# Four K=32 row strips for the gated products of a fused attention and GEGLU kernel, with re-made instruction tables

## The chip, the cores and the metric

One core of one Trainium2 chip. The metric is device time of one execution in microseconds. All runs quoted are of the fast state; on one core, executions of one kernel mostly agree within 0.3%. A ratio of two kernels is the mean time of the fast runs of one over the mean of the fast runs of the other in the same rounds on the same chip, so it is not quite the ratio of the medians quoted beside it.

## The reference, cut to what matters

```python
# x: 4 x 12416 x 128, inducing: 32 x 128
h = mab(I, x)            # 32 rows attend to all of x: h is 32 x 128 for each of 4 batches
y = mab(x, h)            # every x row attends to the 32 rows of h: y = a @ h, a is 12416 x 32
# then on the 49664 rows of y:
ffn = (gelu(y @ w_gate) * (y @ w_val)) @ w_out      # 128 -> 1536 -> 128
out = y + sigmoid(y @ w_res) * ffn
```

Since y = a @ h with only 32 columns in a, the kernel never forms y for the first layer: it computes h @ w_gate and h @ w_val once per batch (32 x 1536 each) and multiplies the attention weights a with them. So the inner dimension K of the large products is 32.

## The kernel before

A *slot* is 512 tokens x 2 chunks of 128 hidden columns: two gate halves (each one matmul with 512 columns into a `g` bank), two value halves (into a `v` pair of banks), two gelus on ACT, and one multiplication on DVE that gives `u` (1,024 columns). Six slots make a group of 512 tokens. TensorE (PE) then multiplies `u` with w_out in 48 small matmuls, called f here, into the single `f` bank. 146 slots make a batch, four batches the kernel. While batch b runs, the exponentials, sums and first layer of batch b+1 run in the background, in slots 90 to 125 or so.

Partitions 0 to 31 and 32 to 63 of the weights both hold the gate copy, 64 to 127 the value copy twice. Before, one product used two copies at once (K=64), and the scales 0.5 and 0.25 undid the doubling:

```python
def emit(gate, value):              # one gate half and one value half
    todo = []
    if gate is not None:
        gb = bank_g()               # 3 banks
        todo.append(products(*gate, slice(0, 64), gb))
    if value is not None:
        ...                         # v: two pairs of banks
        todo.append(products(i, h, slice(64, 128), v_t[i][:, h * TOK:(h + 1) * TOK]))
    ...                             # the matmuls, in turn; then gelu (ACT), and after the 2nd half u (DVE)
```

The mixes (R: input of the sigmoid, written as tanh; A: the residual) used half the height:

```python
pe.matmul(bank[...], rt_t[...][rows, ...], hra_t[self.b][rows, :])    # rows = 0:64 or 64:128
```

The order of all this is a table of words, one word a slot. P: the two value halves with two gate halves; Q: with one gate half; V: without; G: one gate half alone; a number: so many f matmuls; R, A: mixes; E: 16 blocks of exponentials; c, h, t, l, r, o: other steps of the next batch. A star at a row's end makes ACT copy the f bank (and GpSimd, POOL, do the rest); without a star DVE does `(th + 1) * f` from the bank. Two rows of the middle table, before:

```python
"8P9 P R10P QE4 EE23EEEcE2cP cQG2",
"GP9 P A8P QG8 2GP 11PA *",
```

The softmax here doesn't subtract the row's maximum and nothing guards it: scores larger than these inputs give would overflow.

## Time and profile before

| | before |
|---|---|
| median of 3 runs | 802.83 us (801.81 to 803.2) |
| first u starts, last u starts | 38.1, 796.3 us |
| the four batches (first u to first u, the last to its last u) | 201.1, 190.0, 189.9, 177.2 us |

The batch times are read from the starts of the u instructions in the trace. The first batch contains a hole near 143 to 151 us. The page's lines are shown in the prediction. ACT's records are about 0.64 us long but can start every 0.477 us, so ACT can be 99% "busy" and still be late.

### The profile page before, as it was taken

The numbers are of one execution on the slowest core, as the hardware profiler recorded it, in microseconds if no ns is written. First come the engines' busy times: TensorE is split into PE (matmuls) and PEld (weight loads), VectorE is DVE, ScalarE is ACT, GpSimd is POOL, SyncE is SP. The second block draws the span as 40 slices with busy tenths as digits, with TensorE's granted clock in tenths as the row PEclk, the third lists the DMA queues.
The fourth block names the chain that finished last, engine by engine and source line by source line (L and its number), as shares of the span: only waits on it lengthen the run. The fifth ranks groups of instructions, "written<-read, shape, count | busy, mean of one in ns | idle before, by whom it ended". The sixth has DMA issues, their size and how long they took to land.

```text
span 801.7 us, 23912 instructions
## 1 busy us (share of the span) xinstructions
PE 771.1 (96%) x9590; PEld 477.3 (60%) x9590; DVE 736.4 (92%) x714; ACT 771.8 (96%) x1528; POOL 518.7 (65%) x504
## 2 busy tenths in 40 slices
PE   5899999699999999999999999999999999999997
PEld 4556556465665656565666655566666565565655
DVE  7799999389899999979899999997989999999997
ACT  7799999599999999999999999999999999999997
POOL 0338998533888999852587999971388683433545
PEclk9999999799999999999999999999999999999999
DMA  9315579411044657710025565651014441101111
GB/s 349 97 44 137 148 183 199 78 45 41 28 98 99 148 145 177 193 61 28 28 74 97 130 149 148 188 122 39 29 35 100 89 96 41 40 28 41 40 41 45
DMA packets 118449, 78.16 MB, mean 97 GB/s; under 512 B 96672, under 2 KB 99392, under 8 KB 118336
## 3 DMA queue, kind: packets, MB, share of 16 engines
q1 hardware_dynamic: 118336, 76.62, 37.2%
q8 instruction: 75, 1.23, 0.7%
q14 instruction: 38, 0.31, 0.1%
HBM read 27.87 MB, written 25.43 MB: 66 GB/s over the span
## 4 chain that ended last, share of the span: by engine, by line
PE 72%; ACT 19%; issue 4%; DMA 2%; DVE 2%; POOL 1%; SPq 0%; DVEq 0%; POOLq 0%; ACTq 0%
PE f L389 31%; PE g L352 28%; ACT ge L358 12%; PE g L397 5%; PE v L352 3%; ACT at L408 1%; ACT xt L142 1%; DMA xf<-in_x_dram 1%; DVE u L366 1%; ACT e L167 1%; ACT fe L417 1%; PE g L163 1%; ACT th L403 1%; PE g L181 1%; ACT hi L117 1%
## 5 line engine op out<-in xcount | busy, mean ns | idle before, releaser
L366 DVE TENSOR_TENSOR u<-ge,v 128x1024 bf16<-128x1024 f32 x584 | 679.1, 1212 | 39.3 <-PE v L352 20.9
L358 ACT ACTIVATE ge<-g 128x512 f32<-128x512 f32 x1164 | 609.3, 641 | 5.4 <-PE v L352 2.1
L352 PE MATMUL g<-rt,hgv 64*128 64x512 f16 x1152 | 360.1, 380 | 3.0 <-DVE nacc L191 0.4
L389 PE MATMUL f<-wO,u 128*128 128x128 bf16 x4656 | 358.7, 221 | 3.0 <-DVE th L421 1.3
L352 PE MATMUL v<-rt,hgv 64*128 64x512 f16 x1152 | 359.4, 383 | 0.0
L389 PEld LDWEIGHTS <-u 128*128 128x128 bf16 x4656 | 265.9, 98 | 134.6 <-issue 119.7
L352 PEld LDWEIGHTS <-hgv 64*128 64x128 bf16 x2400 | 124.8, 93 | 112.2 <-issue 36.2
L422 POOL TENSOR_TENSOR at<-at,th 128x512 f32<-128x512 f32 (+1 forms) x100 | 123.9, 1240 | 81.8 <-ACT ge L358 48.6
L418 POOL TENSOR_TENSOR th<-th,fe 128x512 f32<-128x512 f32 (+1 forms) x58 | 70.6, 1218 | 118.9 <-ACT fe L417 118.7
L293 POOL TENSOR_TENSOR a<-e,z 128x1024 f16<-128x1024 f32 (+1 forms) x48 | 89.7, 1878 | 14.6 <-DVE z L279 9.7
L397 PE MATMUL g<-hra,rt 64*128 64x128 f16 x768 | 73.2, 216 | 8.7 <-ACT e L167 7.6
L397 PEld LDWEIGHTS <-rt 64*128 64x128 f16 x768 | 51.1, 94 | 47.1 <-issue 27.2
L125 POOL TENSOR_TENSOR lo<-xf,hi 128x1024 f16<-128x1024 f32 x36 | 76.9, 2136 | 0.3
L419 POOL TENSOR_TENSOR at<-at,fe 128x512 f32<-128x512 f32 (+1 forms) x58 | 70.6, 1218 | 0.0
L408 ACT ACTIVATE at<-g 128x512 f32<-128x512 f32 (+1 forms) x100 | 61.8, 618 | 0.3 <-issue 0.2
L403 ACT ACTIVATE th<-g 128x512 f32<-128x512 f32 (+1 forms) x100 | 61.7, 618 | 0.4
L119 POOL CAST hi<-xf 128x1024 f16<-128x1024 f32 x36 | 37.4, 1038 | 14.0 <-DMA xf<-in_x_dram 11.2
L417 ACT ACTIVATE fe<-f 128x512 f32<-128x512 f32 (+1 forms) x58 | 36.0, 621 | 2.1 <-PE f L389 2.0
L421 DVE SCALAR_TENSOR_TENSOR th<-th,f 128x512 f32<-128x512 f32 x42 | 28.6, 681 | 1.6 <-POOL a L272 1.6
L163 PEld LDWEIGHTS <-xt 128*128 128x128 f16 x768 | 23.3, 97 | 8.0 <-issue 3.9
L206 POOL CAST hra<-hf 64x128 f16<-64x128 f32 x4 | 1.1, 288 | 40.4 <-DVE hf L201 30.1
L167 ACT ACTIVATE e<-g 128x512 f16<-128x512 f32 (+1 forms) x36 | 18.5, 613 | 8.0 <-POOL a L293 7.9
(112 smaller groups left out, 281.1 us busy)
## 6 DMA issues: line engine op xcount, KB each, us to landing
out_dram<-at SPq DMA_DIRECT2D x96, 256.0 KB, 2.0
xf<-in_x_dram SPq DMA_DIRECT2D x38, 512.0 KB, 4.3
ge<-in_x_dram SPq DMA_DIRECT2D x10, 512.0 KB, 7.8
rt<-a SPq DMA_TRANSPOSE x48, 3.1
xt<-hi SPq DMA_TRANSPOSE x36, 3.4
ge<-in_moe_w_gate_dram SPq DMA_DIRECT2D x1, 512.0 KB, 8.8
ge<-in_moe_w_val_dram SPq DMA_DIRECT2D x1, 512.0 KB, 8.9
ge<-in_moe_w_out_dram SPq DMA_DIRECT2D x1, 512.0 KB, 4.3
```

Of the source, the lines that this page charges most:

```text
L125: eng.tensor_tensor(lo[:, :w, :P], xf_t.pop((b, k))[:, :w, :], hi_t[b, k][:, :w, :], AL.subtract)
L293: eng.tensor_tensor(a2[:, :n], ev[:, o:o + n, :].unsqueeze(2).to_broadcast([P, n, Q, M]), z[:, o:o + n].unsqueeze(2).unsqueeze(3).to_broad ...
L352: pe.matmul(*t[n], start=True, stop=True)
L358: act.activation(ge_t[i][:, h * TOK:h * TOK + n], gb[:, :n], AC.Gelu, bias=0.0, scale=1.0)
L366: ve.tensor_tensor(u[:, :n], ge_t.pop(i)[:, :n], v_t.pop(i)[:, :n], AL.mult)
L389: pe.matmul(self.ffn[:, k, :], u_t[self.gi, si][:, o:o + P], wO[:, fc, :], start=first, stop=not self.todo, skip_group_check=True)
L397: pe.matmul(bank[:, k * P:(k + 1) * P], rt_t[self.b, self.k][rows, self.j0 + k, :], hra_t[self.b][rows, :], start=True, stop=True)
L403: act.activation(self.th[:, :self.tw], self.mix(slice(0, 64)), AC.Tanh, bias=0.0, scale=0.5)
L408: act.activation(self.at[:, :self.tw], self.mix(slice(64, 128)), AC.Copy, bias=0.0, scale=1.0)
L418: po.tensor_tensor(th, th, fe, AL.mult)
L419: po.tensor_tensor(at, at, fe, AL.add)
L422: po.tensor_tensor(at, at, th, AL.add)
```

## The change

The intent: use each copy once. With K=32 four products on four different row strips can run in the array at once, where two ran before. The scales double, the mixes use all 128 rows with zeros in the unused ones (the same array mode as the f matmuls), and the tables were made anew for the lighter PE, with 35 stars in place of 58.

```diff
-    def products(i, h, rows, bank):
+    def products(i, h, strip, bank):
+        rows = slice(strip * M, (strip + 1) * M)          # M = 32
...
-    def emit(gate, value):
+    def emit(value, ngate):
         todo = []
-        if gate is not None:
-            gb = bank_g()
-            todo.append(products(*gate, slice(0, 64), gb))
         if value is not None:
+            v = v_t[value] = bank_v()
+            for h in range(len(halves_of(value))):
+                todo.append(products(value, h, 2 + h, v[:, h * TOK:(h + 1) * TOK]))
+        for _ in range(ngate):
+            ...
+                gb = bank_g()
+                todo.append(products(*gate, sent["g"] % 2, gb))
... (matmuls in turn, then u on DVE, then the gelus on ACT)
-        hra = p_h.tile([P, P], FP16, ...)
+        hra = p_h.tile([P, 2, P], FP16, ...)               # two versions, each with 64 zero rows
...
-    pe.matmul(bank[...], rt_t[...][rows, ...], hra_t[self.b][rows, :])
+    pe.matmul(bank[...], rt_t[...][:, ...], hra_t[self.b][:, s, :])
...
-                at(8 * i - 4, lambda i=i: weights_b(0, i))
-            for i, j in zip((16, 46, 80), later):
+                at(6 * i - 2, lambda i=i: weights_b(0, i))
+            for i, j in zip((14, 38, 62), later):
... (all three tables; the row of the middle table with the first exponentials:)
-        "8P9 P R10P QE4 EE23EEEcE2cP cQG2",
+        "R9GQ 19EEEV VE EE6EccQ G9P 7VGG6 *",
```

More of the change, by code (lines that the diff above doesn't have):

```diff
@@ L199, in finish_h @@
         ve.reciprocal(rz, hs[:, P:P + 1])
-        hf = p_h.tile([P, P], FP32, name="hf", tag="hf", bufs=1)
+        hf = p_h.tile([P, P + 1], FP32, name="nacc", tag="nacc", bufs=1)[:, :P]
         ve.tensor_scalar(hf, hs[:, 0:P], rz, None, op0=AL.mult)
         hf_t[b] = hf
-        hra = p_h.tile([P, P], FP16, name="hra", tag="hra")
+        hra = p_h.tile([P, 2, P], FP16, name="hra", tag="hra")
         hra_t[b] = hra
-        po.tensor_copy(hra[2 * M:, :], hf[2 * M:, :])
-        po.tensor_tensor(hra[3 * M:, :], hf[3 * M:, :], hra[3 * M:, :], AL.subtract)
+        po.memset(hra[2 * M:, 0, :], 0.0)
+        po.memset(hra[:2 * M, 1, :], 0.0)
+        po.tensor_copy(hra[2 * M:, 1, :], hf[2 * M:, :])
+        po.tensor_tensor(hra[3 * M:, 1, :], hf[3 * M:, :], hra[3 * M:, 1, :], AL.subtract)
         hgv_t[b] = p_h.tile([P, F], BF16, name="hgv", tag="hgv")
@@ L236, in first_layer_t @@
         act.activation(hgt_t[b][:, s].rearrange("p c m -> p (c m)"), bank[:, :FCH * M],
-                       AC.Copy, bias=0.0, scale=(0.5, 0.25)[s])
+                       AC.Copy, bias=0.0, scale=(1.0, 0.5)[s])
     def spread(b, c0, c1):
@@ L252, in res_layer @@
         hra = hra_t[b]
-        act.activation(hra[:64, :], bank[:64, :P], AC.Copy, bias=0.0, scale=1.0)
-        ve.tensor_tensor(hra[M:2 * M, :], bank[M:2 * M, :P], hra[M:2 * M, :], AL.subtract)
+        act.activation(hra[:64, 0, :], bank[:64, :P], AC.Copy, bias=0.0, scale=1.0)
+        ve.tensor_tensor(hra[M:2 * M, 0, :], bank[M:2 * M, :P], hra[M:2 * M, 0, :], AL.subtract)
     def sums_b(b, j0, j1, eng):
@@ L336 @@
     v_t = {}
-    def emit(gate, value):
+    def emit(value, ngate):
         todo = []
-        if gate is not None:
-            gb = bank_g()
-            todo.append(products(*gate, slice(0, 64), gb))
         if value is not None:
-            i, h = value
-            if h == 0:
-                v_t[i] = bank_v()
-            todo.append(products(i, h, slice(64, 128), v_t[i][:, h * TOK:(h + 1) * TOK]))
-        for n in range(max(map(len, todo))):
+            v = v_t[value] = bank_v()
+            for h in range(len(halves_of(value))):
+                todo.append(products(value, h, 2 + h, v[:, h * TOK:(h + 1) * TOK]))
+        gates = []
+        for _ in range(ngate):
+            gate = gate_half()
+            if gate is not None:
+                gb = bank_g()
+                todo.append(products(*gate, sent["g"] % 2, gb))
+                gates.append((gate, gb, len(todo[-1])))
+        for n in range(max(map(len, todo), default=0)):
             for t in todo:
@@ L352, in emit @@
                     pe.matmul(*t[n], start=True, stop=True)
-        if gate is not None:
-            i, h = gate
+        if value is not None:
+            gi, si = flat[value]
+            n = groups[gi][4][si][1] * groups[gi][3] * P
+            u = p_u.tile([P, 2 * TOK], BF16, name="u", tag="u")
+            ve.tensor_tensor(u[:, :n], ge_t.pop(value)[:, :n], v_t.pop(value)[:, :n], AL.mult)
+            u_t[gi, si] = u
+        for (i, h), gb, n in gates:
             if h == 0:
                 ge_t[i] = p_ge.tile([P, 2 * TOK], FP32, name="ge", tag="ge")
-            n = len(todo[0]) * groups[flat[i][0]][3] * P
+            n *= groups[flat[i][0]][3] * P
             act.activation(ge_t[i][:, h * TOK:h * TOK + n], gb[:, :n], AC.Gelu,
                            bias=0.0, scale=1.0)
-        if value is not None:
-            i, h = value
-            if h == len(halves_of(i)) - 1:
-                gi, si = flat[i]
-                n = groups[gi][4][si][1] * groups[gi][3] * P
-                u = p_u.tile([P, 2 * TOK], BF16, name="u", tag="u")
-                ve.tensor_tensor(u[:, :n], ge_t.pop(i)[:, :n], v_t.pop(i)[:, :n], AL.mult)
-                u_t[gi, si] = u
     class Last:
@@ L392, in mms, with mix @@
                     del u_t[self.gi, si]
-        def mix(self, rows):
+        def mix(self, s):
             bank = bank_g()
             for k in range(self.nk):
-                pe.matmul(bank[:, k * P:(k + 1) * P], rt_t[self.b, self.k][rows, self.j0 + k, :],
-                          hra_t[self.b][rows, :], start=True, stop=True)
+                pe.matmul(bank[:, k * P:(k + 1) * P], rt_t[self.b, self.k][:, self.j0 + k, :],
+                          hra_t[self.b][:, s, :], start=True, stop=True)
             return bank[:, :self.tw]
@@ L402, in gate @@
             self.th = p_fin.tile([P, TOK], FP32, name="th", tag="th", bufs=3)
-            act.activation(self.th[:, :self.tw], self.mix(slice(0, 64)), AC.Tanh,
+            act.activation(self.th[:, :self.tw], self.mix(0), AC.Tanh,
                            bias=0.0, scale=0.5)
@@ L407, in residual @@
             self.at = p_fin.tile([P, TOK], FP32, name="at", tag="at", bufs=3)
-            act.activation(self.at[:, :self.tw], self.mix(slice(64, 128)), AC.Copy,
+            act.activation(self.at[:, :self.tw], self.mix(1), AC.Copy,
                            bias=0.0, scale=1.0)
@@ L449 @@
     make_identity(nc, ident)
-    ve.memset(parts[:64, :], 0.5)
-    ve.memset(parts[64:, :], 0.25)
+    ve.memset(parts[:64, :], 1.0)
+    ve.memset(parts[64:, :], 0.5)
     ve.tensor_copy(identF, ident)
@@ L553 @@
     plan_first = [
-        "P GP GP8 GP8 P6 P9",
-        "PR8 P4A 5P P9 RP8 P6 *",
-        "P6 RP6A Q2 P11 AP13 P2 *",
-        "3P 12P5 P13R P11 P2 7P",
-        "R9P 8P A11P A4P 4P9 PA *",
-        "8P 7P 5P 11RP 11P6 P7",
-        "P8 GP8 P4G 4Q P3RA6 P",
-        "6P8 AP9 3PG 13P G5P 6P",
-        "9PR 9P8 1PA 10P P11 RP13",
-        "GP13 PR9 2QA P9G P9 P8R",
-        "P 12P G10QAG 2P 7P 8PG",
-        "8P4 1P7 P4GG 7QA QR9G P9",
-        "P5 P7 RP9 PG9 P A3P",
-        "6P8 PA8 P 7P 16EEEVEE 15P *",
@@ L568 @@
-        "R20Q P13 RP7 5Pc P5 P7",
-        "AP9 P4 P6 AR5Q P10G GccEE13cP *",
-        "9P 6P7 P3 cP9 PA9 P7 *",
-        "P6 QAR1 5hP11 tP5 P8 PR10",
-        "P4 P10 PA8l 3Q RP9 GP8 *",
-        "P 6P 6AP7 P12 PR 13Q",
-        "P17EEE VE2EEE 16P Q 16P 8P",
-        "R8P 8PA 8olP R6P6 P7 PA *",
-        "7P 5P7 P10 PA13 oP6 PR6 *",
-        "P5 P7 oPo11R P11 P11r P8",
-        "GP10 AP8 *",
+        "GGQGG GVG4 P6 P4 GV R8VG",
+        "G5GQG 7AQ6 RP8A GP6 GQ2 4GQ *",
+        "7P8G Q8 GQ13R P8 4P 5Q",
@@ new lines @@
+        "R7P 8P10 AA6GP 4GQ7 P8 P10",
+        "GGGV 9GQ2G 8RP 1P7 P A8P7G",
+        "Q 13GP 12P Q8GG 7P3 1Q",
+        "R5PA P11 P4 A9V GP5GG 6P",
+        "8P 5A4P QR 10PR 10GP QA14",
+        "P11 QG8 GGV6 GG9RQG 5GQ9 GQ9",
+        "GVG 7GVGR9 GQA9GG Q 5P5G VR10",
+        "P10 P 18EV VEE2Ac cQ5 P *",
+        "10GQ7GG Q7G GV6G Q11AG Q12 P7G",
+        "V G6P4R 7P 6P G6GP Q4R7 *",
+        "P7G Q4A4 V GA9GGV 13PG 7Q",
+        "6GP6 P7 P7G Q8 RR7P A8P",
+        "8GQ 8GQ9A 3P8 R4GQG1 5P6 QG7",
@@ L579 @@
+        "GVG7G Q7A 4P5 R6GP2 GQ7 GQ7GG",
+        "V17EE E15EcP 6cP Q9AR4 P5 GVA7G",
+        "Q6 GGV11 GGcP Q8R P7G P7 *",
+        "QG7 GQ6R 5QG 8hP 4P6A 5GtQ",
+        "QG9l G1QG 6Q G4A7P 6P lGV5RR",
+        "8P 7P7rG V 21EEAV EEEEVE6 9PG17",
+        "GoQ6 QG8 R2GQoG 5VGG 6P5A 6P *",
+        "R8VG G6GVG 12oPG11 oGQ7 GQ5 2P7",
+        "GVG 7A4P5G *",
     ]
     plan = [
-        "RQ P5GA7 PA7 P6 P6 PR *",
-        "6P 6P 6P11 AP2 9P 6P7 *",
-        "PR 7P 6P 11RP11 P6 P2",
-        "5PA 6P 9PG 9P QA11R P10 *",
@@ L585 @@
-        "P 8P1 6P 12PA 11P 10PR *",
-        "9P 5P 13PR10 P3 P7 PA6 *",
-        "P 6P 6P10R P12 P 5P7 *",
-        "PA7 P6 P1 10P A11P 4P7 *",
-        "PR 5P5 2P5 P9 RP11 P *",
-        "6P7 PA7 P6 P11 AP8 3P7",
-        "P6 PR6 P9 PA1 8P P11R",
-        "P 8P 8P 11P A10P P14",
-        "GP10 P8 P4 1P5R G6P R6P *",
-        "5P10 PA3 6P5 P13R P1 10P6 *",
-        "P8 2P A9P12 AP 12P 9PR",
-        "8P9 P R10P QE4 EE23EEEcE2cP cQG2",
-        "GP9 P A8P QG8 2GP 11PA *",
-        "8P 8PR 8P3 cP3 P 10P",
@@ L599 @@
-        "R11PA11 P R13P cP1 6PA 9P *",
-        "9P R8hP 4P 11P A11tQ Pr14",
-        "EVEEEEE7E Q 16Q P6R A5P6 P7",
-        "P3 l4P 7PG7 l3PA 6P2 4P9 *",
-        "PR9 oP5 P7 o6AP 12P 6P9 *",
-        "PoR10 P11 oAP11 P5 P7 P8",
-        "GP9R P8 *",
+        "AP Q7R 5AP8G Q5 1QG5 GQ5R *",
+        "6V GG6P 12GQ G4Q6 P7G P",
+        "6GVG6 P7 RQ5RA 7VGGG5 P7 GQ7G *",
+        "Q8 RQA8 P4 Q9 PA13G VG",
+        "9QG11 GQ2 8A5RP 1P 7GQ7G QA7G *",
+        "Q7 GQ7G VG12 GP12 P 7P7",
+        "GV G7P 8RR7GP VG8G P8 P8A",
@@ new lines @@
+        "1P6 P6 GQ6A 5P P10R 3QG",
+        "9P 9QG10GG 7P P 8RP7 P *",
+        "6QG5 GVG8 AQA14 GQ4 P 6P *",
+        "7PR 7P1 5P 9RP 9GP V12",
+        "P7 A5VGG8G Q7 P6GR 3GV P12GG",
+        "Q6 7GQ8 GQ7 RA8GP 6P8 P9",
+        "GQ7 A6QG8R 4GQ GV5GG 7GQ 7GQ8R",
+        "2P6 P8A 5AP 4GQ 8GQ 8GQ",
+        "R9GQ 19EEEV VE EE6EccQ G9P 7VGG6 *",
+        "A2Q A8P 7QG3 cP6R 2P7 P8",
+        "P8 P7 GQ10AR cP3 P7G Q6",
+        "GG6P 7VGG8G Q11GGc GV2 R3P6Gh GVG2G",
+        "Q10A2 1GQ8G Q8AR 6tP1 GGV 7GVG8A",
@@ L606 @@
+        "1VG R7P7 GGV17E EV VEE1 EE10EP",
+        "Qo30G V G7lGVG VGG6lR 6P7GG V6",
+        "QoG4 3GVG8 AR8GV GPo7GGo5A 6P6 P7",
+        "GQ 8RQ2 GG7rGV G2P11 GQG10 P7",
+        "P8 P5A5 *",
     ]
     plan_last = [
-        "RQAR 3P 9PG 8P6 1P 6P",
-        "8P R9P A10Q P4 GA6P 6P *",
-        "8PG7 1P 7PR 9Q P14 AP9 *",
-        "P5 P1 7P6 6PR12 P5 P7 *",
-        "AP7 P6 P11 AP 12P5 P7 *",
-        "RP 6P7 P11 RP11 P6 P3 *",
-        "4PA 7P5 P12 AP11 P6 P7",
-        "PR6 P 9P A9P P9 RP9 *",
@@ L616 @@
-        "P6 AP7 P6 P11 RP13 P5 *",
-        "P5 7P 5P 13P 4P 9PR8",
-        "P7 P 10P A10P P9R P9 *",
-        "P6 AP 7P 6P 11GP12 P5",
-        "P7 PR 7P 7P A10PR V *",
-        "A9AP 13P R9P 6P 11P G10Q *",
-        "P11 AP5 5P6 P11R P11 P7",
-        "P 5P 8RP 9PA 8P P *",
-        "10AP 10P6 P9 PG 13P Q13 *",
-        "RP9 P6 P8 P2 10PR 11P *",
-        "10AP10 P2 2P3 10RP11 P 7P9 *",
-        "PA 11P Q10G P12 P5 P7A",
-        "P 7P 7P4RR 6Q P 12AP9 *",
-        "P7 AP9 P11R P11 P6 P6 *",
@@ L630 @@
-        "P8 GP8 P5 Q4R P 14P *",
-        "10P 10PA 14Q P14G P 13P",
-        "RVA21G GPGG *",
+        "AP Q5 R7PR2 Q1 A12P 7VGG *",
+        "8P 8GP 10P Q7A6 Q R7P5 *",
+        "P5G 3QG 3GV12 GQG12 P4A VG4",
+        "QR 9P R10GQ A9P GGQ 10QG *",
+        "11GQ8 P7 GQ3R 9Q P13 AP7 *",
+        "P6 2P9 P6 R5P Q13 2P",
+        "9P4 4GVG8R A8P G3P 6P6 A3P1G",
+        "Q6G Q6 P4G Q6GG 7P A1P *",
+        "7P8 P5R 7P 8VGG 12Q P6 *",
+        "R7P7 GGV10 VGGA6 5VG G7P Q13",
+        "GGV8 GVG8A 4GQ 9RQ G6GGQ Q8AR *",
@@ new lines @@
+        "7VGG 11P10 P12 GP V 10AQA8",
+        "QG4 1GP7 Q R8PG 10P P6R",
+        "8P10 P10 P10A 4P P3R 10P",
+        "9P10 QG10 RA6GV GQ7 GG8GVG8G Q6 *",
+        "P6 GQ7 6PG 10QR8 QG7GG V6 *",
+        "QG9 AQ8 P G11P 4P 7P",
+        "7PR 9P A10GQG VG7R 4P3 3QG",
+        "6GQG 6QG4 VGG8 RGQ1A 6P GV7RA *",
+        "8P9 QG10 GQ14 GP 7Q7 P8A4 *",
+        "GQ 8P 14V GP11R GQ5 P6A5 *",
+        "P7 GQ5 1PG 8Q P6 6P4 *",
+        "A7GQ 7RQ2 R7P4 5GQG V13 P7 *",
+        "A6GQ8 GVG6 Q8G GQ15 GQ11G Q10",
@@ L633 @@
+        "GQRA12GG GGGPGG *",
     ]
@@ L677 @@
     on_act = [row.endswith("*") for b in range(B) for row in table(b)]
-    def single():
-        g = gate_half()
-        if g is not None:
-            emit(g, None)
     def gate_half():
@@ L751 @@
                 if t in "PQV":
-                    for h in range(len(halves_of(i))):
-                        emit(gate_half() if t == "P" or (t == "Q" and h == 0) else None, (i, h))
+                    emit(i, "VQP".index(t))
                     sent["v"] += 1
                 elif t == "G":
-                    single()
+                    emit(None, 1)
                 elif t.isdigit():
```

## The prediction

> **What bounds the kernel now.** I read the page first: engine shares, chain of waits, costliest groups.
>
> ```profile
> PE 771.1 (96%) x9590; PEld 477.3 (60%) x9590; DVE 736.4 (92%) x714; ACT 771.8 (96%) x1528; POOL 518.7 (65%) x504
> ...
> PE 72%; ACT 19%; issue 4%; DMA 2%; DVE 2%; POOL 1%; SPq 0%; DVEq 0%; POOLq 0%; ACTq 0%
> ...
> L366 DVE TENSOR_TENSOR u<-ge,v 128x1024 bf16<-128x1024 f32 x584 | 679.1, 1212 | 39.3 <-PE v L352 20.9
> L358 ACT ACTIVATE ge<-g 128x512 f32<-128x512 f32 x1164 | 609.3, 641 | 5.4 <-PE v L352 2.1
> L352 PE MATMUL g<-rt,hgv 64*128 64x512 f16 x1152 | 360.1, 380 | 3.0 <-DVE nacc L191 0.4
> L389 PE MATMUL f<-wO,u 128*128 128x128 bf16 x4656 | 358.7, 221 | 3.0 <-DVE th L421 1.3
> ```
>
> Three engines look full, and the chain runs mostly through PE. "Busy" does not settle it: neighbouring instructions overlap, so an engine can be covered by records and still start them late. So I took the distance from one start to the next out of the trace. ACT, 512 columns: never below 0.474 us, median 0.477 (gelu to gelu, mean 0.502). DVE, one u: lower quartile 1.131, mean 1.228. PE, timeline of one slot (a slot is one u of 1,024 columns: two gate halves, two value halves, about eight f matmuls):
>
> ```profile
> 298.45 0.56 PE L389 MATMUL f<-wO,u 128*128 128x128 bf16 x7
> 298.95 0.39 PE L352 MATMUL g<-rt,hgv 64*128 64x512 f16 x1
> 298.95 0.39 PE L352 MATMUL v<-rt,hgv 64*128 64x512 f16 x1
> 299.17 0.38 PE L352 MATMUL g<-rt,hgv 64*128 64x512 f16 x1
> 299.18 0.38 PE L352 MATMUL v<-rt,hgv 64*128 64x512 f16 x1
> 299.49 0.28 PE L389 MATMUL f<-wO,u 128*128 128x128 bf16 x2
> ```
>
> Here g and v start together (3 ns apart in the trace), the second pair 0.22 us later, the next f 0.308 us after the last v. Over the trace f follows f after 0.056 us, g follows f after 0.151, f follows v after 0.308, with hardly any spread from 640 to 780 us: PE rarely waits there. It is full of its own work.
>
> Last, the windows (ordinary stretch, background stretch, last batch) and the waits of the one hole:
>
> ```profile
> 240.00:340.00 100.00, 98.96 (x1080) 59.60 (x1079) 97.10 (x87) 99.52 (x203) 88.86 (x76) 1.00 0.64 154
> 340.00:400.00 60.00, 59.33 (x936) 38.36 (x935) 51.39 (x54) 59.32 (x114) 27.00 (x29) 1.00 0.12 39
> 640.00:780.00 140.00, 138.88 (x1535) 83.98 (x1533) 136.21 (x121) 139.35 (x282) 68.44 (x54) 1.00 0.15 45
> ...
> ACT e L167 <- POOL a L293: 7.9, 1, 7.9
> PE g L397 <- ACT e L167: 7.6, 1, 7.6
> ```
>
> Columns are PE, PEld, DVE, ACT, POOL. In the background stretch (exponentials and sums of the next batch) DVE falls to 51 of 60 us while PE and ACT stay full. The two waits are the hole around 143 to 151 us in the first batch.
>
> **What the Trainium skill says.** "TensorE: Matmul & The Clock Gate", Part 3, "Measured speedup vs the span model": four row tiles of K=32, N=512 ran 3.07 times as fast, one starting some 4 ns after another. The trace agrees for two strips of 64 (3 ns); no run yet shows four. "TensorEngine Tiling (Array Packing)", "Key Properties": changing the tiling mode, unlike changing the tile, drains TensorE. The trace agrees: 0.151 instead of 0.056 into K=64, and 0.308 instead of one stream (0.216) out of it, so about 0.095 + 0.092 = 0.19 us for each excursion. The same page, "Gotcha 1: PSUM Pressure": different row tiles need different PSUM banks. Here g has three banks and v two pairs, so four strips take two of three g banks at once. "ScalarE: Activation LUTs", "What ACT_TABLE_LOAD costs": 186 + 0.833 N ns less 93 of overlap, an estimate of 520 ns for 512 columns; the trace has 477, which I use. Its table load of 1283 ns is what the page has.
>
> **The change, part by part.** K=64 was half waste: each product was made twice from copies and halved by the scales. Now K=32, scales doubled, up to four halves in one pass of the array.
>
> PE. I counted the word tables (middle table twice), writing out each unbroken run of products between f and mix matmuls. Before: 558 runs, 1,221 passes. After: 564 runs, 664 passes, if products on different strips always share a pass, also where a G stands beside a Q or V. 557 passes fewer at 0.22 us are 123 us of PE work. Mixes at full height no longer switch mode when they stand among f matmuls: 74 + 119 such transitions in the trace at 0.093 us are 18 us at most. Against that I allow 0.05 us a run for four weight loads ahead instead of two: 28 us.
>
> Per middle batch PE needed before: f 1,164 x 0.056 = 65.2; runs 139.5 x 0.189 = 26.4; passes 305 x 0.218 = 66.5; mixes 194 x 0.056 = 10.9, their switches 4.6; background about 12 (estimate: 194 exponential matmuls at 0.025, sums, switches). Sum 185.6, and the batch took 190 (first u's at 239.2, 429.2 and 619.1 us). Four batches, the last without background: 730. After: 65.2 + 36.2 + 26.6 + 7 + 10.9 + 2 + 12 = 160, four batches 628.
>
> ACT. Gelus and mixes stay: (291 + 50) x 0.477 = 162.7 a batch. The stars (f copied by ACT, two more POOL additions) fall from 10, 15, 15, 18 to 6, 7, 7, 15, that is 58 to 35. Exponentials 14 x 0.477 = 6.7, table loads 6 or 4 at 1.294 (as many as before, by counting the E runs), small ones 1.1. Before 183.1 + 2 x 182.9 + 171.3 = 720; after 181.2 + 2 x 179.0 + 169.9 = 709.
>
> DVE. u stays: 145 x 1.131 + 0.6 = 164.6 a batch. Each star dropped puts a 0.598 us operation here: 15, 10, 10, 7 become 19, 18, 18, 10. Background 4 a batch. Before 696; after 180.0 + 2 x 179.4 + 170.6 = 709.
>
> POOL loses 23 x 2 x 1.27 = 58 us. That lies beside other work, except at the hole. There the fifth exponential needs one of three e buffers, held until weights_b of tile 11, scheduled at slot 84 and run late behind a full POOL (38.8 of 40 us busy from 80 to 120). After, that weights_b stands at slot 64, and the exponential that needs the buffer comes at slot 102. I expect the hole to close: 12 slots took 27.5 us there against 14.6 usual plus 5 of exponentials and tables, so 8 us, 10 with the restart.
>
> **Sum.** First u at 38.1 us and tail after the last u 5.4 us stay. The stretch between was 758, without the hole 748, over the tightest engine's 730: 97.6%. After, PE drops out (628) and ACT and DVE bind at 709 each. Two equal bounds that feed each other work a little worse than one, so I take 97%: 731. Total 38.1 + 731 + 5.4 = 774.5, rounded 774: 28 us or 3.5% less. Of these about 10 are the hole, and 18 are the bound that moves from PE to ACT and DVE; the 100 us of PE that go are mostly not on the path afterwards.
>
> **Rivals.**
> 1. PE was not the bound, ACT and DVE were. For it: ACT busy 99.5 of 100 us, and 720 of work in 748 is nearly as tight as PE. Then efficiency is 720/748 = 96.3%, or less with the two balanced at 709 (95%): 709/0.95 + 43.5 = 790. Against it: PE's steady gaps, and the loss in the background stretches, where PE's extra work is largest.
> 2. A new wait for g banks. Two gates at once take two of three banks, a mix a third, and PE, in order, holds f and v behind them. For it: three g banks, ACT 0.64 us per gelu until its bank is free. Against it: v goes first in a P, and PE has some 0.3 us of slack a slot to wait in. If 0.02 to 0.04 us a slot appear on ACT or DVE: 12 to 23 us, so 786 to 797.
> 3. Four strips do not run together, or separated G's do not merge. If only two do, the passes saved vanish and PE is again at 730: 790 to 800. Against it: two strips start 3 ns apart here.
> 4. The hole stays, moved: E's now start at slot 62 and need tiles 4 and 5 turned, scheduled by slot 55, with POOL by my sum 1.07 times loaded there. 5 to 10 us more: 780 to 784.
> 5. Better than thought: with PE loose both reach 99%: 760.
>
> **Range and chances.** Rivals 2 and 4 in part and 5 span 761 to 789, my 8 in 10. The 2% line is 786.8. Rivals 1 and 3 in full or 2 at its worst cross it: faster 0.85, within 2% 0.13, slower 0.02 (only if new tables stall PE on banks every slot).
>
> **What would show it.** Right: four starts within about 30 ns in the timeline, one K=32 excursion of about 0.45 us a slot against 0.63; the chain of waits going from PE 72% to under half, ACT and DVE taking it; PE's waits for ACT or DVE appearing where there were none; gelu to gelu mean near 0.49; u to u near 1.17 to 1.20; slot rate in ordinary stretches 1.18 to 1.20 us against 1.22; middle batches 184 to 186 us against 190, first about 187 against 201; no ACT wait of 8 us on POOL. Wrong: PE still most of the chain with steady gaps (rival 3); v or g waits on ACT that leave DVE idle by more than 5% (rival 2); a hole in the first batch (rival 4); middle batches unchanged though PE has slack (rival 1).

## The result, and the profile after

Correct. Median of 4 runs 774.85 us (774.73 to 775.65) against 802.79 for before; ratio 0.9656, 95% interval 0.9639 to 0.9673. The batches took 188.8, 184.6, 184.5 and 171.0 us, the first u again started at 38.3 us and the last at 767.3.

The page of the changed kernel, the lines that answer to those of before (busy shares; chain of waits; groups with busy time, mean ns and idle time before):

```profile
PE 736.8 (95%) x9590; PEld 431.0 (56%) x9590; DVE 742.4 (96%) x737; ACT 754.2 (98%) x1505; POOL 462.5 (60%) x466
...
ACT 43%; PE 39%; issue 11%; DVE 5%; DMA 1%; POOL 1%; SPq 0%; ACTq 0%; POOLq 0%; DVEq 0%
...
L362 DVE TENSOR_TENSOR u<-ge,v 128x1024 bf16<-128x1024 f32 x584 | 670.6, 1212 | 10.3 <-PE v L357 2.7
L368 ACT ACTIVATE ge<-g 128x512 f32<-128x512 f32 x1164 | 609.1, 657 | 2.7 <-PE g L357 1.2
...
L357 PE MATMUL g<-rt,hgv 32*128 32x512 f16 x1152 | 335.9, 379 | 9.3 <-ACT ge L368 0.6
L357 PE MATMUL v<-rt,hgv 32*128 32x512 f16 x1152 | 222.9, 385 | 2.5 <-DVE u L362 1.6
```

The chain that ended last now runs through ACT (43%) more than PE (39%), against 72% PE before. DVE's idle time before u fell from 39.3 to 10.3 us. PE still reads 95% busy, which again says little: waiting matmuls hide in overlapping records.

The timeline of PE in the changed kernel, one slot:

```profile
294.73 0.28 PE L391 MATMUL f<-wO,u 128*128 128x128 bf16 x2
294.94 0.38 PE L357 MATMUL g<-rt,hgv 32*128 32x512 f16 x1
294.94 0.39 PE L357 MATMUL v<-rt,hgv 32*128 32x512 f16 x2
294.95 0.39 PE L357 MATMUL g<-rt,hgv 32*128 32x512 f16 x1
```

All four products start within 10 ns: one pass where the slot before needed two. In the trace an f follows the last product after 0.304 us in the median, as before (0.308), so four strips cost no more than two. An unhindered slot costs PE 0.095 + 0.01 + 0.304 = 0.41 us beside its f matmuls, against 0.095 + 0.003 + 0.222 + 0.003 + 0.308 = 0.63 before.

The windows of the changed kernel (PE, PEld, DVE, ACT, POOL busy), an ordinary stretch, one of background work, one in the last batch:

```profile
240.00:340.00 100.00, 97.53 (x1190) 56.06 (x1190) 98.76 (x92) 99.89 (x203) 78.76 (x69) 1.00 0.59 150
340.00:400.00 60.00, 59.18 (x925) 36.00 (x922) 57.15 (x63) 59.66 (x119) 23.36 (x37) 1.00 0.13 39
640.00:750.00 110.00, 106.47 (x1221) 59.83 (x1219) 109.98 (x101) 109.90 (x224) 37.67 (x30) 1.00 0.11 38
```

In the second line DVE is busy 57.15 of 60 us where it had 51.39. Part of that is the window itself, for the changed kernel is ahead by then: its background stretch of this batch (slots 90 to 126) runs from 335.6 to 385.3 us, that of before from 349.8 to 404.1. Counted by slots, DVE is busy 46.4 us there in both kernels, in 54.3 us before and in 49.6 now. In the last batch DVE is now full (109.98 of 110).

Where does that come from? DVE's timeline around the first exponentials of a middle batch, before:

```profile
352.70 2.34 DVE L366 TENSOR_TENSOR u<-ge,v 128x1024 bf16<-128x1024 f32 x2
357.92 0.30 DVE L188 COPY nacc<-g 128x129 f32<-128x129 f32 x1 [2.87 <-PE g L183]
358.88 0.29 DVE L191 TENSOR_TENSOR nacc<-g,nacc 128x129 f32<-128x129 f32 x1 [0.67 <-PE g L183]
359.50 1.22 DVE L366 TENSOR_TENSOR u<-ge,v 128x1024 bf16<-128x1024 f32 x1 [0.33 <-PE v L352]
```

and after:

```profile
336.92 0.69 DVE L423 SCALAR_TENSOR_TENSOR th<-th,f 128x512 f32<-128x512 f32 x1
338.42 2.35 DVE L362 TENSOR_TENSOR u<-ge,v 128x1024 bf16<-128x1024 f32 x2 [0.81 <-PE v L357]
341.44 0.29 DVE L187 COPY nacc<-g 128x129 f32<-128x129 f32 x1 [0.66 <-PE g L182]
342.00 0.29 DVE L190 TENSOR_TENSOR nacc<-g,nacc 128x129 f32<-128x129 f32 x1 [0.27 <-PE g L182]
```

While ACT loads tables and does seven exponentials (353.7 to 359.5 and 336.7 to 342.4), there is no gelu for some 5.7 us. Before, no value product stood among the exponentials, and DVE had no u to do: 5.67 us from one u to the next. After, two V words stand among them; DVE works off u's whose gelus had been done ahead, and the longest distance there is 2.81 us.

### The profile page after: what moved, and what is told of

The parts are those of the page before. It is cut to its first block, busy times and chain, and to the rows that moved or that the text cites. A ratio compares the mean times of both kernels' runs of the same rounds, so it can differ in the third digit from the quotient of the medians.

```text
span 773.1 us, 23909 instructions
## 1 busy us (share of the span) xinstructions
PE 736.8 (95%) x9590; PEld 431.0 (56%) x9590; DVE 742.4 (96%) x737; ACT 754.2 (98%) x1505; POOL 462.5 (60%) x466
## 4 chain that ended last, share of the span: by engine, by line
ACT 43%; PE 39%; issue 11%; DVE 5%; DMA 1%; POOL 1%; SPq 0%; ACTq 0%; POOLq 0%; DVEq 0%
ACT ge L368 29%; PE f L391 18%; PE g L357 10%; PE v L357 6%; ACT th L405 3%; ACT at L410 3%; DVE u L362 3%; PE g L399 3%; ACT e L166 2%; ACT xt L141 1%; ACT fe L419 1%; ACT L166 1%; ACT hi L116 1%; ACT L368 1%; DMA ge<-in_x_dram 1%
## 5 line engine op out<-in xcount | busy, mean ns | idle before, releaser
L362 DVE TENSOR_TENSOR u<-ge,v 128x1024 bf16<-128x1024 f32 x584 | 670.6, 1212 | 10.3 <-PE v L357 2.7
L357 PE MATMUL g<-rt,hgv 32*128 32x512 f16 x1152 | 335.9, 379 | 9.3 <-ACT ge L368 0.6
L357 PE MATMUL v<-rt,hgv 32*128 32x512 f16 x1152 | 222.9, 385 | 2.5 <-DVE u L362 1.6
L357 PEld LDWEIGHTS <-hgv 32*128 32x128 bf16 x2400 | 73.7, 91 | 87.8 <-issue 24.2
L420 POOL TENSOR_TENSOR th<-th,fe 128x512 f32<-128x512 f32 (+1 forms) x35 | 41.3, 1180 | 94.4 <-ACT fe L419 94.4
L294 POOL TENSOR_TENSOR a<-e,z 128x1024 f16<-128x1024 f32 (+1 forms) x48 | 89.7, 1880 | 12.3 <-DVE z L280 7.8
L399 PE MATMUL g<-hra,rt 128*128 128x128 f16 x768 | 71.3, 219 | 2.5
L399 PEld LDWEIGHTS <-rt 128*128 128x128 f16 x768 | 50.7, 97 | 16.1 <-issue 13.1
L423 DVE SCALAR_TENSOR_TENSOR th<-th,f 128x512 f32<-128x512 f32 x65 | 44.4, 683 | 2.5 <-PE g L162 1.8
L421 POOL TENSOR_TENSOR at<-at,fe 128x512 f32<-128x512 f32 (+1 forms) x35 | 41.3, 1179 | 0.0
L419 ACT ACTIVATE fe<-f 128x512 f32<-128x512 f32 (+1 forms) x35 | 22.1, 631 | 0.9 <-PE f L391 0.9
L273 POOL TENSOR_TENSOR a<-a 128x256 f32<-128x256 f32 (+5 forms) x45 | 18.6, 413 | 3.5
```

The lines of the kernel that those rows point to most:

```text
L294: eng.tensor_tensor(a2[:, :n], ev[:, o:o + n, :].unsqueeze(2).to_broadcast([P, n, Q, M]), z[:, o:o + n].unsqueeze(2).unsqueeze(3).to_broad ...
L357: pe.matmul(*t[n], start=True, stop=True)
L362: ve.tensor_tensor(u[:, :n], ge_t.pop(value)[:, :n], v_t.pop(value)[:, :n], AL.mult)
L399: pe.matmul(bank[:, k * P:(k + 1) * P], rt_t[self.b, self.k][:, self.j0 + k, :], hra_t[self.b][:, s, :], start=True, stop=True)
L420: po.tensor_tensor(th, th, fe, AL.mult)
L423: ve.scalar_tensor_tensor(th, th, 1.0, f, AL.add, AL.mult)
```

## The experiments

Twelve kernels ran. The first eight separate code, tables, schedule, stars, mixes and word order; the last four relieve one engine at a time. The table is the summary; "middle" is the first of the two middle batches in the profiled run (the second lies within 0.7 us of it). On total time, the other columns, all runs of a kernel count.

| run | median us | ratio to before (95%) | middle us |
|---|---|---|---|
| before | 802.8 to 803.5 | 1 | 190.0 |
| changed kernel | 774.85 | 0.9656 (0.9639 to 0.9673) | 184.6 |
| old code, new tables | 825.27 | 1.0274 (1.0258 to 1.0289) | 197.7 |
| new code, old tables | 805.98 | 1.0025 (0.9995 to 1.0054) | 189.9 |
| changed, only two strips | 811.01 | 1.0095 (1.0076 to 1.0114) | 190.3 |
| before, weights_b earlier | 797.83 | 0.9927 (0.9897 to 0.9956) | 190.0 |
| changed, old stars | 800.03 | 0.9958 (0.9934 to 0.9983) | 191.4 |
| new code, old tables, new stars | 819.72 | 1.0204 (1.0180 to 1.0228) | 195.5 |
| changed, half-height mixes | 790.94 | 0.9850 (0.9833 to 0.9867) | 187.6 |
| changed, merged words | 776.24 | 0.9672 (0.9649 to 0.9694) | 184.8 |
| before, half of A on ACT | 798.69 | 0.9944 (0.9922 to 0.9965) | 188.6 |
| new code, old tables, half of A on ACT | 797.41 | 0.9928 (0.9909 to 0.9948) | 187.8 |
| changed, half of A on ACT | 769.59 | 0.9581 (0.9556 to 0.9606) | 182.8 |
| changed, half of th*f on DVE | 774.58 | 0.9646 (0.9624 to 0.9668) | 184.3 |

### Code and tables apart

Old code with the new tables and schedule. Old code gives one gate with each value half; the last slot of a batch has one half only, so one G had to be added to keep the count of gates (without it the kernel does not build):

```diff
 before.py, all three tables, weights_b and sums slots of the changed kernel, and:
+                    if t == "P" and len(halves_of(i)) == 1:
+                        single()
```

> The code of before (K=64, two products at a time, mixes at half height) with the new tables and the earlier weights_b. My theory (PE was the tightest engine, 730 us of own work in the 748 us between first and last u without the hole): the hole goes, PE stays the bound, 788 to 798 us. Rival 1 (PE was no bound; fewer stars and the closed hole are the whole gain): 774 to 780 us. An outcome between says both count.

Measured: 825.27 us, slower than either parent, and past both expectations. Its page:

```profile
PE 86%; ACT 9%; issue 2%; DVE 2%; DMA 1%; POOL 1%; SPq 0%; POOLq 0%; DVEq 0%; ACTq 0%
```

The new tables on the old products make PE the bound: 86% of the chain. My expectation had overlooked why: with two strips a word like GQ or VGG takes three passes where a P takes two. Counted from the tables, the old code needs some 1,420 passes with the new tables, against 1,221 with its own. So this run does not show the tables alone; it shows them with some 200 passes (at 0.22 us) more on PE.

New code with the old tables. The new code takes u's gate halves from earlier words, so the first word issues two gates ahead (without that it does not build):

```diff
 after.py, all three tables, weights_b and sums slots of before, and:
-        "P GP GP8 GP8 P6 P9",
+        "GGP GP GP8 GP8 P6 P9",
-                    emit(i, "VQP".index(t))
+                    emit(i, min("VQP".index(t), len(halves_of(i))))
```

> The new code (four strips, mixes at full height) with the tables and weights_b slots of before; only the first word differs (the first two gates are issued ahead, since value now comes before gate). My theory: PE is relieved (about 628), ACT with its 58 stars binds at 720: 720/0.97 + 43.5 + 8 for the hole, so 786 to 796 us. Rival 1: no gain from PE, 799 us or more. If the hole of about 8 us on POOL shows again in this trace, it belongs to the old slots of E and weights_b.

Measured: 805.98 us, middle batches 189.9. My theory failed here: relieving PE alone, with everything else as it was, gained nothing in a middle batch (the last batch, without background, went from 177.2 to 175.3). The four runs lie between 802.45 and 807.73 us; the profiled one is the fastest, and the two longest have the lowest granted clocks (0.979 and 0.981 against 0.988). So a gain or loss of 2 us in the total is not to be read here. The hole showed again (ACT waits 7.5 us for POOL), as expected of the old slots. The windows of this run:

```profile
240.00:340.00 100.00, 96.70 (x1078) 52.70 (x1077) 97.35 (x88) 99.71 (x204) 89.24 (x76) 1.00 0.66 155
340.00:400.00 60.00, 56.08 (x939) 36.18 (x937) 51.45 (x54) 59.01 (x114) 27.23 (x31) 1.00 0.12 39
```

DVE and ACT stand where they stood before (97.10 and 99.52, 51.39 and 59.32); only PE has less. The u gap at the first exponentials is 5.74 us here, as in the kernel before: it belongs to the old tables. From the distances between PE's starts I added up what exceeds the unhindered distance: some 23 us in a middle batch before, some 37 here. That is where the freed PE time went: into waits, most of them ended by a gelu that gave its g bank back. These sums depend on which distance is called unhindered, above all at half-height mixes: recounted from the traces with other choices they are 13 to 28 us before and 39 to 45 here. The direction is sure, the size is not.

### Four strips or two, all else as changed

```diff
-                todo.append(products(value, h, 2 + h, v[...]))
+                todo.append(products(value, h, 2, v[...]))
-                todo.append(products(*gate, sent["g"] % 2, gb))
+                todo.append(products(*gate, 0, gb))
 (and issued value, gate, value, gate, so that two still run at once)
```

> The changed kernel, but both value halves use strip 2 and all gates strip 0, issued value, gate, value, gate: at most two K=32 products run at once, ACT, DVE, POOL, tables and mixes as changed. My theory: PE is back at some 715 to 730 us, 787 to 798 us. Rival 1: 774 to 780 us, since PE had slack before too.

Measured: 811.01 us, 36 more than the changed kernel, against some 13 to 23 expected. So the packing is indispensable to the new tables, which with two strips need 1,307 passes, counted as in the prediction, against 664 with four and 1,221 before. The middle batches lost 5.7 and 5.8 us, the last 8.3, the first 16.3. Some 11 us of the first are of another kind: its first 24 slots took 41.2 us against 30.1, while PE's clock was granted at half speed from 41.8 to 69.1 us. This is discussed with the mixes below.

### The hole

```diff
 before.py:
-                at(8 * i - 4, lambda i=i: weights_b(0, i))
-            for i, j in zip((16, 46, 80), later):
+                at(6 * i - 2, lambda i=i: weights_b(0, i))
+            for i, j in zip((14, 38, 62), later):
```

> The kernel before with only weights_b at slots 6i-2 and the sums at 14, 38 and 62 in place of 8i-4 and 16, 46, 80. My theory: the e buffer that the fifth exponential waits for is free in time, the 7.9 us wait of ACT on POOL goes, 793 to 796 us. Rival: POOL is full there, the earlier multiplications only push the conversions back and the stall moves to the transposed x: 799 us or more.

Measured: 797.83 us, in four runs between 794.54 and 800.50. ACT's timeline at the fifth exponential, before:

```profile
150.51 0.60 ACT L167 ACTIVATE e<-g 128x512 f16<-128x512 f32 x1 [7.92 <-POOL a L293]
```

and in this run:

```profile
147.41 0.60 ACT L167 ACTIVATE e<-g 128x512 f16<-128x512 f32 x1 [2.42 <-PE g L163]
```

The wait for the e buffer is gone, as I had it. A shorter one took its place: PE waits 2.6 us for a DMA transpose of x. Both explanations hold in part; how much the total gained is uncertain, as the four runs spread over 6 us. The slots 72 to 84 took 27.5 us before, 24.0 here. In the changed kernel they take 14.4: there the exponentials were moved as well, to slots 62 and 102.

### The stars

```diff
 after.py: the stars of rows as in before.py (58 in place of 35), words unchanged
```

> The changed kernel with the 58 stars of before instead of its 35 (23 more f copies on ACT, 23 fewer 0.598 us operations on DVE), all else as changed. My theory (ACT and DVE are both at their bound, 709 each): ACT's own work becomes 720, so 720/0.973 + 43.5, 781 to 786 us, middle batches 187 to 189. Rival (the order of the tables is what counts, the balance has slack): 774 to 777 us.

```diff
 new code with old tables, as above: the stars of the new tables (35 in place of 58), words unchanged
```

> As the run of the new code with the old tables, but with the 35 stars of the new tables in place of 58. That run stood at 190 us a middle batch although PE was relieved. If ACT's load was what held it: ACT's middle batch falls from 182.9 to 179.0, so 186 to 187 us a middle batch and 794 to 797 us in all, the hole staying. If the order of the old tables holds it, whatever the load: 189 to 190 a middle batch and 803 to 807 us.

Measured: 800.03 and 819.72 us. Both moves of stars cost far more than the work they shift (23 operations of 0.477 us on ACT against 0.598 us on DVE): 25 us one way, 14 the other way. None of my expectations, for either run, foresaw this. The waits of the first run, and of the changed kernel for comparison:

```profile
DVE u L362 <- ACT ge L368: 14.4, 27, 1.2
...
PE g L357 <- ACT ge L368: 7.5, 14, 0.6
...
PE f L391 <- DVE th L423: 6.4, 12, 1.0
```

```profile
DVE u L362 <- ACT ge L368: 1.8, 5, 0.7
...
PE f L391 <- ACT fe L419: 1.1, 3, 0.5
```

and of the second run:

```profile
ACT ge L368 <- PE g L357: 24.6, 48, 1.2
...
PE f L391 <- DVE th L423: 19.1, 37, 1.0
```

against, in the new code with the old tables and their own stars,

```profile
ACT ge L368 <- PE g L357: 3.4, 12, 0.5
...
PE f L391 <- DVE th L423: 0.7, 2, 0.4
```

There is one f bank. Who empties it, ACT or DVE, decides when PE may begin the f matmuls of the next group, and everything behind them in PE's order waits too. The f counts in a table's words are set for the star of that very group. So these two runs do not measure the balance of ACT and DVE, as I had meant them to; they show that stars and words belong together. The reason is read from the waits; no run tried it alone. Of the 14 us of the second run some may be the clock: its trace has half-speed stretches inside the middle batches too (369.8 to 376.6 and 564.3 to 567.7 us), where the run that it is compared with has none.

### The mixes

```diff
-                pe.matmul(bank[...], rt_t[...][:, self.j0 + k, :], hra_t[self.b][:, s, :], ...)
+                pe.matmul(bank[...], rt_t[...][64 * s:64 * s + 64, self.j0 + k, :],
+                          hra_t[self.b][64 * s:64 * s + 64, s, :], ...)
```

> The changed kernel with its mixes at half height (K=64) again, reading the same rows without the zero rows. My theory: up to 18 us of PE work come back, but PE has slack now: 774 to 778 us. Rival (each change of tiling mode costs wall time): 785 us or more.

Measured: 790.94 us, 16 more: the rival was right. Three us of each middle batch and 2.6 of the last are the ordinary cost of the mode changes. The first batch lost 7.6, and again part of it is the granted clock. The windows of the changed kernel (the column before the DMA share is the clock):

```profile
42.00:46.00 4.00, 3.83 (x33) 2.07 (x33) 3.60 (x4) 3.43 (x7) 0.18 (x1) 0.75 0.40 70
46.00:50.00 4.00, 3.95 (x45) 2.24 (x45) 3.70 (x4) 4.00 (x9) 0.00 (x0) 1.00 0.01 4
50.00:54.00 4.00, 3.88 (x41) 1.82 (x39) 3.92 (x5) 4.00 (x9) 3.12 (x2) 1.00 0.17 66
```

and of this run:

```profile
42.00:46.00 4.00, 4.00 (x32) 2.23 (x33) 3.15 (x3) 2.98 (x6) 0.29 (x1) 0.50 0.35 70
46.00:50.00 4.00, 4.00 (x29) 2.01 (x24) 2.66 (x3) 3.06 (x6) 0.00 (x0) 0.50 0.02 4
50.00:54.00 4.00, 3.86 (x29) 1.90 (x27) 3.13 (x4) 3.41 (x7) 1.23 (x2) 0.50 0.00 0
```

The changed kernel itself spends 40.6 to 44.0 us at half clock, this run 40.9 to 58.0 and again 88.7 to 92.1, the two-strip run 41.8 to 69.1. The kernel before and the old code with the new tables have no such stretch after their first u (the only later one of before begins in its hole). Of all 14 traces, eight of the ten with K=32 products have a half-speed stretch in the first 10 us or so after the first u, and none of the four with K=64 products. The two exceptions are the runs that relieved one engine of the changed kernel, so in this code it can fall either way. By the Trainium skill, "TensorE: Matmul & The Clock Gate", Part 1, "What's actually happening", activity of PE over a window of 3.4 us sets whether it gets half or full clock. The lengths here agree with such a window (3.41, 17.07 and 27.31 us are 1, 5 and 8 times 3.41). That the K=32 products count as less activity than the K=64 ones fits these runs; none of them tests it.

### The order inside a slot

```diff
 after.py, all tables: each GVG, GGV, VGG, GQ, QG that stands alone becomes P
```

> The changed kernel with its tables coarsened: every GVG, GGV, VGG, GQ and QG that stands alone becomes a P (value first, then two gates), so the same products in the same passes, f counts, stars and mixes, only the order of gate and value inside a slot is lost. If the order inside a slot is not what pays (my theory, as four strips run in one pass either way): 774 to 778 us. If it pays, because a gate put first gets its g bank earlier and ACT waits less: 780 us or more.

Measured: 776.24 us. Inside a slot the order of gate and value counts for 1.4 us at most; products that stand together share a pass, in whatever order they come. So what is special in the new tables is not the place of a G inside its slot; gates issued ahead of their slot were left as they were.

### One engine relieved at a time

To ask which engine holds a kernel, I took work from ACT alone (A on half of the columns, POOL clearing the rest: 25 x 0.213 = 5.3 us a batch) in three kernels, and from DVE alone in one. Their outputs are wrong, which doesn't matter for the times. The last one still passes the comparison.

```diff
-            act.activation(self.at[:, :self.tw], self.mix(...), AC.Copy, ...)
+            hw = self.tw // 2
+            po.memset(self.at[:, hw:self.tw], 0.0)
+            act.activation(self.at[:, :hw], self.mix(...)[:, :hw], AC.Copy, ...)
```

> Wrong results on purpose. The kernel before, but ACT copies only half the columns of each residual mix (POOL clears the other half): 25 x 0.213 = 5.3 us less ACT work a batch, same PE and DVE work and order. New theory (before was held by ACT: 182.9 us of work and some 7 us of late starts in a 190 us batch): middle batches 184 to 186, 779 to 787 us in all. My old theory (PE the tightest): 188 to 190 a middle batch, 796 to 803 us.

> Wrong results on purpose. The same ACT relief in the run of the new code with the old tables, where PE has slack. New theory: ACT holds it, so middle batches 184 to 186 from 189.9, some 21 us less in all, 782 to 788 us. If this gains clearly more than the same relief in the kernel before, PE is close behind ACT there.

> Wrong results on purpose. The same ACT relief in the changed kernel. If ACT and DVE both hold it (179.0 and 179.4 us a middle batch in 184.6), relief of ACT alone gives little: 182 to 184.6 a middle batch, 765 to 775 us. If ACT alone holds it: 179 to 180 a batch, 753 to 758 us.

```diff
-                ve.scalar_tensor_tensor(th, th, 1.0, f, AL.add, AL.mult)
+                hw = tw // 2
+                ve.scalar_tensor_tensor(th[:, :hw], th[:, :hw], 1.0, f[:, :hw], AL.add, AL.mult)
```

> Wrong results on purpose. The changed kernel with DVE's multiplication by f on half the columns: 0.267 us less for each of 65, 4.8 us a middle batch, 17 in all, on DVE alone. If both engines hold it: 182 to 184.6 a middle batch, 766 to 775 us. If DVE alone holds it: 180 a batch, 757 to 760 us.

Measured: 5.3 us less of ACT work gave a middle batch 1.4 us before, 2.1 with the new code and the old tables, 1.8 in the changed kernel; 4.8 us less of DVE work gave the changed kernel at most 0.3. The last two totals, 769.59 and 774.58, are what I had expected if ACT and DVE both hold the changed kernel. My second theory, that ACT alone held the kernel before, fell as the first had: with PE and ACT both relieved a middle batch still takes 187.8 us, where the new tables reach 184.6 with no less ACT work than that run had (179.0 against 182.9 less 5.3, 177.6). In that run the stretch of the exponentials is unchanged:

```profile
340.00:400.00 60.00, 56.09 (x945) 36.72 (x942) 51.73 (x55) 58.38 (x114) 29.64 (x39) 1.00 0.13 41
```

DVE 51.73 of 60 us, against 51.39 before. Of the 2.1 us that ACT's relief gave there, 1.3 lie in the ordinary stretch and 0.3 in that of the exponentials. From the starts of u, a middle batch divides so (mean of the two):

| us for | slots 0 to 90 | slots 90 to 126 (background) | slots 126 to 146 |
|---|---|---|---|
| before | 110.6 | 54.3 | 25.1 |
| new code, old tables | 109.9 | 54.5 | 25.5 |
| the same, half of A | 108.6 | 54.1 | 25.0 |
| changed, two strips | 111.6 | 51.8 | 26.9 |
| old code, new tables | 116.0 | 54.0 | 27.7 |
| changed | 108.4 | 49.6 | 26.5 |

Of the 5.4 us that a middle batch gained, 4.7 lie in the background stretch, 2.2 in the ordinary one, and 1.4 are given back at the end. No relief of PE or ACT moved the background stretch by more than 0.3 us under the old tables. The changed kernel with two strips, so the new tables and mixes without the packing, already took 2.4 us off it, and with four strips it is 2.2 more. With the old code the new tables took only 0.3 off it, though the same V words stand among their exponentials and the longest distance from u to u there is 2.89 us.

These stretches do not hold equal work for ACT, though. Between slots 90 and 126 the changed kernel starts 63 gelus where before had 69, one mix and one f copy less, 3.8 us in all at 0.477; six of these gelus come after slot 126 instead, which is about the time given back. So the 4.7 us are in part work that moved out of the stretch. Over a whole middle batch ACT starts 371 instructions instead of 377, mainly the f copies dropped: some 3 us, and its late starts fall by some 2.5 us more. That the 3 us alone would not have come out is shown by the run with half of A under the old tables: ACT has less work there than in the changed kernel, and the batch still takes 187.8 us.

## Why the prediction was right or wrong, point by point

**The time and the sum: right.** 774.85 against 774; the stretch between first and last u 729 us against 731. The floor of ACT and DVE, 709 each, and 97% on it, held batch by batch: 188.8 against 187, 184.6 and 184.5 against 184 to 186, and a last batch of 171.0 where DVE alone needed 170.6. That it came within 1 us is in part luck: the 97% was carried over from PE's 730 us in 748, and PE was not the bound. Set against ACT's 720 the efficiency before was 96.3%, and that would have given about 780.

**Four strips in one pass: right.** Four starts within 10 ns, 0.41 us a slot instead of 0.63. The 0.05 us a run that I allowed for weight loads does not show.

**"PE drops out": right after, wrong before.** The step that failed is that PE was the tightest engine, with 730 us of its own work, so that loosening it would free the rest. It had waits of some 23 us (13 to 28 by the recounts) in a middle batch that took 190, so 162 to 177 us of own work, not the 185.6 that I had added up, and less than ACT's 182.9. (Part of the excess: I counted a change of mode for every run of products, also where a half-height mix stood beside it and no mode changed. The rest I have not traced.) Relief of PE alone gave a middle batch 0.1 us. I had read "the gaps of PE are steady" as "PE never waits", but the waits sat in the distances between products, which I had not summed. In its place: three in-order engines, each near its limit, with three g banks, two v pairs and one f bank between them. Under the old tables neither PE nor ACT alone held the kernel, and both relieved gave 2.2 us a middle batch.

**"18 are the bound that moves from PE to ACT and DVE": the size right, the path another.** In ACT's account of a middle batch some 3 us are fewer f copies, as predicted, and some 2.5 are fewer late starts. The better order shows most in the exponentials, where value products placed among them and gelus done ahead feed DVE. The placing alone does not do it (54.0 us with the old code, against 54.3). The packing is what lets PE keep the new order: without it the same tables cost 36 us more.

**Mixes, "18 us at most", "mostly not on the path": mis-sized.** Taking full height away cost 16 us, some 11 from changes of mode and some 5 from the granted clock.

**The hole: right in cause, nearly so in size.** Batch 0 gained 12.3 us, 7 more than the middle ones; I had 8 to 10. The earlier weights_b alone bring 5.7 us (medians), with a shorter wait left; in the changed kernel, where the exponentials moved too, no such wait is left.

**Rivals.** Rival 1 was right that PE was not the bound before, wrong that ACT and DVE at their then efficiency set the time after (790): the new tables raised it. Rival 2 (waits for g banks) is there, some 19 us in a middle batch of the changed kernel (23 to 27 by the recounts), but it falls in PE's slack: ACT's late starts sum to 4.5 us, below the 6.7 of before (6.8 and 9.3 by the recount, so the same fall). Rivals 3 and 4 did not come.

**What stays open.** Which feature of the tables pays in the background stretch: the V words among the exponentials, the larger number of f matmuls beside them, or the gates issued ahead. The timelines speak for the first together with the third; no run tried any of them alone. And no run took work from DVE under the old tables.

## What to carry to other kernels

When several in-order engines each run near their limit through few buffers, the engine that the chain of waits names is not thereby the one to relieve: test it by taking work from it alone, and expect little until the order of issue is re-made for the new costs. Conversely, judge a cheaper instruction together with a schedule made for it; here the code alone was worth nothing, the schedule alone cost 22 us (it gives the old code more passes), and together they were worth 28. In such a kernel look first at the places where one engine changes its task for some microseconds (here table loads and exponentials), and ask what its neighbours have to do meanwhile.

## What the Trainium skill lacked or had wrong

- "TensorEngine Tiling (Array Packing)", "Key Properties", says that a change of tiling mode drains TensorE but gives no cost. The runs show 0.095 us on the way from full height into K=64 or K=32 and 0.088 to 0.092 us on the way back, and 16 us in this kernel for mixes that change mode against mixes that do not, part of it through the clock.
- No page gives the time from the last of several packed products to the next matmul of full height. The runs show that it does not grow from two strips to four: 0.304 us from the last of four to the next f, 0.308 from the last of two.
- "TensorE: Matmul & The Clock Gate", Part 1, "What's actually happening", says that after about 3.4 us of sustained work the clock is full. With half-height mixes PE was 3.86 to 4.00 us busy in each 4 us from 42 to 54 us and was still granted 0.50, in all for 17 us; with two strips for 27 us. (Busy time can hide waits, so how sustained this work was is not fully shown.) The page does not say whether the used rows count as activity.
- "ScalarE: Activation LUTs", "What ACT_TABLE_LOAD costs": the figures there make an estimate of 520 ns from start to start for 512 columns with immediate scale and bias; the trace has 477.
